# Casting loads on one queue, a causal triangle by matmul and a new instruction order in a fused chunk-selecting attention and softplus MLP kernel

## The chip, the core and the metric

The kernel runs on one core of a Trainium2 chip. The core has a matrix engine (PE, the weight loads of which the profile lists apart as PEld), a vector engine (DVE), a scalar engine (ACT), GpSimd (POOL) and a sync engine (SP) that only issues transfers here. POOL issues transfers too, on a queue of its own, and only POOL's transfers change the type of what they move. The engines run side by side, each in its own program order, and wait for one another on semaphores. The metric is the device time of one execution in microseconds, as a median over runs: 267.46 us before the change (three runs, 266.27 to 268.2).

## What is computed

The inputs are q, k, v of shape (4, 8, 768, 64), batch, heads, tokens and width, and two MLP weights of 512 x 2048 and 2048 x 512, all f32. Each head's 768 keys are cut into 24 chunks of 32. A query looks only at the six chunks whose upper bound of the score is largest, among the causal ones:

```python
ub = np.sum(np.maximum(q*k_min, q*k_max), axis=-1)          # per query and chunk
ub = np.where(causal, ub, -1e9)
top_chunks = np.argsort(ub, axis=-1)[..., -6:]
scores = scale * np.matmul(q, k.T)
scores = np.where(sel & (pos[:, None] >= pos[None, :]), scores, -1e9)
attn = softmax(scores);  x = attn @ v                        # heads side by side: 512 wide
h = x @ w_in
out = softplus(h) @ w_out                                    # 3072 x 512, f32
```

## The kernel before, in words

**Blocks.** The 3072 tokens are worked on in 12 blocks of 256 queries, numbered n; a block belongs to batch n // 3 and is the first, second or third part (k = n % 3) of that batch's 768 tokens. The eight heads are four pairs. Everything is bf16 in SBUF.

**Preparation of a block.** k and q are loaded with tokens on partitions and turned so that the width is on partitions (names kT and qT). In blocks 0 to 2 the turning is done by PE against an identity (L468 to L472, by groups of two pairs in block 0); from block 3 on by a transposing DMA on SP's queue (L473). From turned k come the chunk maxima and negated minima (L500, L502, DVE), put into a block-diagonal matrix BD (L505), and the keys themselves copied into KA and KB (L512). Turned q is copied (L535) and split in its positive and negative parts (L543). PE then makes the bounds (L565, name ub), DVE the sixth largest of each row and a raw mask (L588, L602), which is turned (L622 by PE, from block 3 on by DMA) and copied into spare rows of the q tiles (L644), so that the score matmul adds the mask by itself.

**Attention of a block.** For each pair and head, PE makes scores in pieces of two key tiles (L684 to L689), ACT exponentiates a piece into the tile pt (L695), POOL puts zeros above the diagonal of the two diagonal tiles with an affine_select (L703 to L707), PE multiplies by v with an extra column of ones (L712), DVE divides by the sum (L725) into the tile osb, and osb is turned into x: by PE and a copy in blocks 0 to 2 and 11 (L740 to L749), by a transposing DMA in the others (L732).

**MLP of a block.** Eight steps h of eight matmuls (L786, one line for all, L791), each followed by an exponential on ACT, and a logarithm for every two (L796, L801); then 2 x 4 steps y of four matmuls (L814, L816), an eviction to ysb and a store.

**Loads.** Block 0's k and q come as f32 on SP's queue, in halves of four heads, with two neighbouring tokens of a head side by side on one partition (512 bytes in one piece; load_pairs, L344). ACT or DVE then casts each half to bf16. Everything else comes as casting loads on POOL's queue: q, k, v of a block in two loads of 128 tokens (load, L328, pieces of 256 bytes), the weights in four loads each (L372, L381). The loads of block 3 wait for the last part of w_out. The helper in_turn (L460) undoes the pairs' order when the turned tile is copied.

**The order of the work.** Nothing in the instruction order is left to the hardware: a planner writes each engine's program. An operation has a list of engines with costs, inputs, buffers and a key, which is the time by which it is wanted; its due time is the smallest of its key and its successors' due times less its own cost (L144 to L146). The planner then plays the kernel through (L136): on each engine it takes, among the operations that could start within a tolerance of the earliest, the one that is due first. The keys hang on the table a (wanted starts of the blocks' attention), and on offsets for preparation, h, y and loads (PAR, L224). A transfer's landing is reckoned with one running end time per queue (L179 to L186). Buffers are counted in pools (sizes, L244): 8 for loaded q and k, 4 each for pt, osb and x, 2 for turned q.

**Fillers.** Before the weights are there, PE has little to do. keep_awake (L837) puts matmuls of zeros (L852, 128 x 128 by 128 columns) in the gaps of PE's planned program until 45 us or the first y step; they write a bank that nobody reads.

Of the kernel before, what the change touches and what calls it, by code (L numbers as in the profile page):

```python
# [10 lines left out]
BF16 = mybir.dt.bfloat16  # L11
# [52 lines left out]

class Op:
    __slots__ = ("name", "alts", "fn", "deps", "gate", "after", "succ", "alloc", "touch", "key",
                 "rel", "packet", "port", "due", "wait", "eng", "start", "end", "done", "dma", "n", "at", "inst")


class Plan:  # L70
# [5 lines left out]
    def op(self, name, alts, fn, deps=(), alloc=(), touch=(), key=None, dma=None, gate=(), after=(), rel=0.0, packet=19.0, port=False):  # L76
        o = Op()
        o.rel, o.packet, o.port = round(rel), packet, port
# [50 lines left out]
    @staticmethod  # L129
    def home_at(pool, s, e):  # L130
        t = 0.0
        for q, x, dma in pool.ends[s]:
            t = max(t, x + (LANDED[e] if dma else 0 if q == e == "PE" else LAT[q].get(e, 150)))
        return t

    def run(self, par):  # L136
# [7 lines left out]
        for o in reversed(topo):  # L144
            dur = min(c for _, c in o.alts) + (2500 if o.dma else 160)
            o.due = min([o.key] + [s.due - dur for s in o.succ])  # L146
        free = {"PE": 3000.0, "ACT": 2300.0, "DVE": 1000.0, "POOL": 800.0, "SP": 800.0}
        ring, packet = {"SP": 0.0, "POOL": 0.0}, {"SP": 19.0, "POOL": 32.0}
# [3 lines left out]
        while ready:  # L152
# [26 lines left out]
            if o.dma:  # L179
                other = "SP" if e == "POOL" else "POOL"  # L180
                at = max(o.end + (650 if e == "SP" else 1150), ring[e], 2650.0)
                back, part = max(0.0, ring[other] - at), packet[other] / o.packet
                ring[e] = at + o.dma + min(o.dma * part, back)
                ring[other] += min(o.dma, back / part)
                packet[e] = o.packet
                o.done = ring[e] + (450 if o.packet < 100 else 1000)  # L186
                if e == "SP":
                    o.end = max(o.end, ring[e] - 3500)
            else:
                o.done = o.end  # L190
# [4 lines left out]
            for b in o.touch:  # L195
                b.left -= 1
                b.ends.append((e, o.done, bool(o.dma)))
# [22 lines left out]
def dve(n, rate=1.0):  # L220
    return n / (0.96 * rate) + 66


PAR = dict(  # L224
    dmat=3,
    dmaT=450,
    narrow=1,
    l0=1,
    over="soy",
    maskD=3,  # L230
    awake=(1.06, 45.0, 5.7),
    first=(64.42, 64.23, 29.03, 95.39),
    loads=((87.43, 130.15, 71.7), 19.14, (76.86, 12.06, 15.17), 41.22),
    tol={"PE": 0, "ACT": 0, "DVE": 0, "POOL": 2358, "SP": 0},
    alt=636,
    ohd=(229.35, 150.58),
    a=(-46.8, -33.92, -31.03, -0.05, 17.1, 24.77, 54.71, 88.7, 133.12, 175.62, 173.66, 255.42, 297.45, 469.8),
    prep=((77.31, -48.97, -81.43, 46.38), (-8.14, 24.92, -67.86, -43.68), (53.78, -16.07, -58.0, 11.26), (25.03, -41.37, -16.45, 11.23)),
    av=(-0.8, 4.76),
    ot=(12.12, 10.86),  # L240
    hlag=(8.7, 27.7, 34.1, -3.53, 34.9, 33.84, 33.54, 32.2, 25.36, -32.32, 54.03, 77.81),
    ylag=(7.32, 7.87, 25.64, 26.35, 28.67, 47.05, 47.88, 49.45, 10.02, 22.03, 47.36, 37.39),
    ahead=(3.4, 19.67, 10.64, 22.05, 12.72, 9.33, 70.63, 47.4, 103.95),
    sizes=dict(s=2, h=2, y=1, o=1, t=2, xf=2, xp=4, kT=2, io=8, kx=2, q=2, pn=2, ub=2, pt=4, osb=4, x=4, g=2, e=4, ysb=4, mT=2),  # L244
# [3 lines left out]
def make_plan(T, par):  # L248
# [19 lines left out]
    P.op("zero", [("DVE", 80)], lambda e: nc.vector.memset(T.zero, 0.0), key=-100000)  # L268
# [26 lines left out]
    chunk_rows = [P.op("c4", [("POOL", 900)], f4, [r4], key=3000)]  # L295
    mr0, bd0, kb0, vone, ohk = [], [], [], [], {}
# [11 lines left out]
    for k0, k1 in ((0, 1), (1, NBLK)):  # L308
        for h in range(2):
            o = P.op("ohk", [("SP", 450)], lambda e, k0=k0, k1=k1, h=h: rows_of(0, k0, k1, h), oh[k0:k1],  # L310
                     key=par["ohd"][k0] * 1e3, dma=300 * (k1 - k0))
# [16 lines left out]
    def load(nm, n, when, gate=()):  # L328
# [6 lines left out]
        for t in range(NT):  # L335
# [4 lines left out]
                     gate=gate, key=key, rel=key - 2000 if n > 2 else 0.0, dma=950 if n < 3 else 2050, packet=32.0, **new)  # L340
            first = first or o
            ld[nm, n, t] = o

    def load_pairs(nm, n, when):  # L344
# [4 lines left out]
        for g in range(2):  # L349
# [4 lines left out]
                     key=1e3 * when[g], dma=950, packet=29.0, alloc=[st])  # L354
# [6 lines left out]
    def load_rows(nm, n, when):  # L361

        for t in range(NT):
            st = Buf(pool["xf"])
            d = P.op(f"ld {nm}{n}.{t}", [("SP", 560)], lambda e, t=t, st=st: nc.sync.dma_start(out=st.ap, in_=rows(nm, n, t)),
                     key=1e3 * (when + 0.3 * t), dma=1000, alloc=[st])
# [5 lines left out]
    def load_w_in(when):  # L372
        for c in range(4):
# [4 lines left out]
            w_in.append(P.op(f"w_in{c}", [("POOL", 800)], f, key=1e3 * (when + 0.4 * c), dma=2550, packet=173.0, after=w_in[-1:]))  # L378

    def load_w_out(when):  # L380
        for c in range(4):  # L381
# [4 lines left out]
            w_out.append(P.op(f"w_out{c}", [("POOL", 800)], f, key=1e3 * (when + 0.4 * c), dma=2550, packet=173.0,  # L386
# [5 lines left out]
    load_pairs("k", 0, (0.0, l0[0]))  # L392
    if par["l0"] < 2:
        load_pairs("q", 0, (l0[1], l0[2]))
    else:
        load("q", 0, l0[1])
# [4 lines left out]
    for nm, x in zip("kqv", l1):  # L401
        load(nm, 1, x)
    load_w_in(li)
    for nm, x in zip("kqv", l2):
        load(nm, 2, x)
    load_w_out(lo)
    for h in range(2):
        o = P.op("ohk", [("SP", 450)], lambda e, h=h: rows_of(1, 0, NBLK, h), oh, gate=[w_out[3]], key=40000, dma=900)
        for k in range(NBLK):
            ohk[1, k, h] = o  # L410
    kb0.append(P.op("kb0", [("SP", 450)], lambda e: nc.sync.dma_start(out=T.KB[1][0:32], in_=T.KB[0][0:32]), kb0[:1],
                    gate=[w_out[3]], key=40000, dma=600))
# [7 lines left out]
    for n in range(NB):  # L420
# [11 lines left out]
        for gi, ps in enumerate(groups):  # L432
# [14 lines left out]
            by_dma, pairs, qpairs = n >= par["dmat"], n == 0, n == 0 and par["l0"] < 2  # L447
# [20 lines left out]
            def transposes(nm, buf, t, n=n, ps=ps, p0=p0):  # L468
                o = t_of(buf)
                for p in ps:  # L470
                    nc.tensor.transpose(o[:, p - p0, t * 128:(t + 1) * 128],
# [476 lines left out]
```

## Time and profile before

| | us |
|---|---|
| median of three runs | 267.46 |
| the profiled execution, its own time | 266.59 |
| its span, first to last instruction | 264.8 |
| PE busy in it | 255.0 |
| ACT busy | 211.0 |
| DVE busy | 142.5 |
| POOL busy | 110.8 |
| fillers on PE (L852), 243 of them | 22.7 |

The span is what the page and the trace cut up; about 1.8 us of the execution lie around it. "Busy" joins the intervals of an engine's instructions. A matmul's interval includes its way through the array, so a row of short matmuls overlaps itself: its pace is read from how often one starts. A view by windows gives each engine's busy time in a stretch, with the granted clock of PE and the share of the DMA engines. In the timeline an entry in square brackets is the idle time of the engine just before that row, and what ended it. "To landing" is counted from the issue of a transfer until its data are there.

### The profile page before, as it was taken

What the parts mean: (1) busy time and instruction counts of PE and PEld (TensorE: products, weight loads), DVE (VectorE), ACT (ScalarE), POOL (GpSimd) and SP (SyncE); (2) the same over time, 40 slices, a digit from 0 to 9 for tenths busy, and PEclk for the clock granted to TensorE, in tenths of its full rate; (3) what the DMA queues carried; (4) which work ended last, traced back from release to release, by engine and by line L of the source; (5) the groups of instructions that cost most, each with busy time, mean ns of one, the idle gap of its engine ahead of it and who ended that gap; (6) DMA issues with size and microseconds to landing.
All of it is one profiled execution on the core that took longest, in us unless ns stands there. A gap on an engine that the chain in (4) does not pass through costs nothing.

```text
span 264.8 us, 7039 instructions
## 1 busy us (share of the span) xinstructions
PE 255.0 (96%) x2750; PEld 197.2 (74%) x2779; DVE 142.5 (54%) x500; ACT 211.0 (80%) x372; POOL 110.8 (42%) x193
## 2 busy tenths in 40 slices
PE   8698999999999999999999999999999999999995
PEld 8698898768775677788678864777888756887744
DVE  6589961019789667447634596584582164221012
ACT  3589999988687879999687992699997885999900
POOL 8927878798318520543990263401110211310000
PEclk9799999999999999999999999999999999999999
DMA  7996999999999984699699969624440123001022
GB/s 162 161 189 90 181 196 231 155 139 190 149 136 173 132 119 89 115 129 100 73 173 150 117 88 174 173 54 120 45 82 0 42 72 99 10 2 42 0 79 79
DMA packets 114719, 29.87 MB, mean 113 GB/s; under 512 B 104544, under 2 KB 111712, under 8 KB 114688
## 3 DMA queue, kind: packets, MB, share of 16 engines
q0 software_dynamic: 74944, 13.11, 66.5%
q1 hardware_dynamic: 39744, 16.33, 33.0%
q8 instruction: 21, 0.34, 0.6%
q14 instruction: 10, 0.08, 0.1%
HBM read 27.26 MB, written 6.29 MB: 127 GB/s over the span
## 4 chain that ended last, share of the span: by engine, by line
PE 86%; DMA 5%; DVE 3%; ACT 3%; issue 1%; POOL 0%; DVEq 0%; POOLq 0%
PE ph L791 30%; PE py L816 17%; PE pt L816 9%; PE po L717 7%; PE ps L687 5%; PE py L852 4%; PE ps L688 4%; DMA io<-in_k_dram 3%; DMA x<-osb 3%; PE pt L687 2%; PE pt L688 1%; PE pt L570 1%; ACT g L801 1%; PE ph L816 1%; ACT e L796 1%
## 5 line engine op out<-in xcount | busy, mean ns | idle before, releaser
L791 PE MATMUL ph<-x,w_in_sb 128*128 128x256 bf16 x768 | 91.8, 272 | 0.0
L705 POOL TENSOR_SCALAR_AFFINE_SELECT pt<-pt 128x256 bf16<-128x256 bf16 x96 | 39.5, 419 | 112.6 <-ACT pt L695 112.1
L791 PEld LDWEIGHTS <-w_in_sb 128*128 128x128 bf16 x768 | 73.6, 98 | 11.5 <-DMA w_in_sb<-in_moe_w_in_dram 0.5
L695 ACT ACTIVATE pt<-ps 128x512 bf16<-128x512 f32 (+1 forms) x134 | 69.9, 564 | 9.4 <-PE ps L688 8.8
L796 ACT ACTIVATE e<-ph 128x512 f32<-128x512 f32 x96 | 56.3, 606 | 12.5 <-PE ph L791 11.8
L816 PEld LDWEIGHTS <-g 128*128 128x128 bf16 x400 | 37.4, 98 | 31.4 <-ACT g L801 0.5
L816 PE MATMUL py<-w_out_sb,g 128*128 128x512 bf16 x231 | 57.8, 379 | 1.5 <-ACT ysb L258 0.2
L801 ACT ACTIVATE g<-e 128x1024 bf16<-128x1024 f32 x48 | 51.1, 1072 | 1.0
L695 ACT ACTIVATE pt<-pt 128x512 bf16<-128x512 f32 (+1 forms) x58 | 32.4, 584 | 0.6 <-PE pt L688 0.6
L717 PEld LDWEIGHTS <-pt 128*128 128x128 bf16 x672 | 26.8, 97 | 5.1 <-issue 0.6
L259 DVE COPY ysb<-py 128x512 f32<-128x512 f32 x12 | 8.3, 691 | 36.9 <-PE py L816 36.9
L717 PE MATMUL po<-v,pt 128*128 128x65 bf16 x610 | 26.4, 193 | 0.3 <-DVE osb L728 0.3
L816 PE MATMUL pt<-w_out_sb,g 128*128 128x512 bf16 x108 | 26.2, 379 | 0.2
L727 DVE RECIPROCAL rec<-po 128x4 f32<-128x4 f32 x43 | 7.6, 178 | 34.9 <-PE po L717 34.6
L490 DVE TENSOR_REDUCE kx<-kT 128x32 bf16<-128x1024 bf16 x18 | 21.0, 1209 | 8.9 <-DMA kT<-io 8.9
L852 PE MATMUL py<-zero 128*128 128x128 bf16 x243 | 22.7, 245 | 1.1 <-DVE zero L268 1.1
L339 POOL DMA_DIRECT2D v<-in_v_dram x24 | 21.6, 905 | 3.8 <-DMA io<-in_q_dram 1.5
L339 POOL DMA_DIRECT2D io<-in_k_dram x22 | 20.0, 910 | 5.7 <-DMA w_in_sb<-in_moe_w_in_dram 2.2
L339 POOL DMA_DIRECT2D io<-in_q_dram x22 | 19.9, 910 | 0.7 <-PE ph L791 0.6
L728 DVE TENSOR_TENSOR osb<-po,rec 128x256 bf16<-128x256 f32 x43 | 18.2, 424 | 2.7 <-DMA x<-osb 1.3
L852 PEld LDWEIGHTS <-zero 128*128 128x128 bf16 x243 | 18.3, 111 | 1.3 <-DVE zero L268 1.1
L687 PE MATMUL ps<-qa,ka 96*128 96x256 bf16 x71 | 18.3, 273 | 0.7 <-DVE qa L259 0.7
(99 smaller groups left out, 302.5 us busy)
## 6 DMA issues: line engine op xcount, KB each, us to landing
out_dram<-ysb SPq DMA_DIRECT2D x23, 256.0 KB, 2.4
v<-in_v_dram POOLq DMA_DIRECT2D x24, 128.0 KB, 7.6
io<-in_k_dram POOLq DMA_DIRECT2D x22, 128.0 KB, 7.2
io<-in_q_dram POOLq DMA_DIRECT2D x22, 128.0 KB, 7.1
w_out_sb<-in_moe_w_out_dram POOLq DMA_DIRECT2D x4, 512.0 KB, 8.0
w_in_sb<-in_moe_w_in_dram POOLq DMA_DIRECT2D x4, 512.0 KB, 9.6
xp<-in_k_dram SPq DMA_DIRECT2D x2, 256.0 KB, 3.2
xp<-in_q_dram SPq DMA_DIRECT2D x2, 256.0 KB, 6.3
```

The source lines that it names most:

```text
L339: lambda e, t=t: nc.gpsimd.dma_start(out=into(nm, n, t), in_=rows(nm, n, t)),
L490: nc.vector.tensor_reduce(kx.ap[:, :, j].rearrange("d p (t c) -> d t p c", t=NT), kT.ap.rearrange("d p x -> d (p x)").rearrange("d (t p c ...
L687: nc.tensor.matmul(sp.ap[:, 0:QB], kk[0:nr, p, j * 128:(j + 1) * 128], qq, start=True, stop=True)
L695: lambda e, sp=sp, pt=pt, h=h, j=j, w=w: nc.scalar.activation(pt.ap[:, h, j:j + 2].rearrange("k j c -> k (j c)")[:, 0:w], sp.ap[:, 0:w], A ...
L705: nc.gpsimd.affine_select(out=d, in_=d, compare_op=ALU.is_ge, fill=0.0, base=0, channel_multiplier=-1, pattern=[[0, 2], [1, 128]])
L717: nc.tensor.matmul(o[:, u, h], pt.ap[:, h, j, c0:c0 + 128], T.V[i][:, j, 2 * p + h, :], start=(j == 0), stop=(j == t0 + u))
L728: nc.vector.tensor_tensor(osb.ap[0], o[:, :, :, 0:D], osb.ap[1].to_broadcast([128, NT, 2, D]), op=ALU.mult)
L791: nc.tensor.matmul(o[:, j], T.w_in[:, dt, ft * 128:(ft + 1) * 128], x.ap[:, dt], start=(dt == 0), stop=(dt == KDM - 1))
L796: lambda e, hb=hb, eb=eb, f2=f2: nc.scalar.activation(eb.ap[:, f2 * 512:(f2 + 1) * 512], hb.ap, ACT.Exp),
L801: lambda e, eb=eb, g=g, f4=f4: nc.scalar.activation(g.ap[:, f4 * 4:(f4 + 1) * 4].rearrange("f j c -> f (j c)"), eb.ap, ACT.Ln, bias=1.0),
L816: nc.tensor.matmul(yb.ap[:, 0:c1 - c0], g.ap[:, f, u * 128:(u + 1) * 128], T.w_out[:, f, c0:c1], start=(f == 0), stop=(f == KFF - 1))
L852: z.fn = lambda e: T.nc.tensor.matmul(T.pools["y"].homes[0][:, 0:128], T.zero, T.zero, start=True, stop=True)
```

## The change

1. **All q, k, v as casting loads.** Block 0's k and q no longer come through SP and f32 tiles, but on POOL's queue (l0=3). The four casts of block 0 go.
2. **k and q of blocks 0, 1, 2 as token pairs.** One load of 1024 pieces of 512 bytes (written as 256) takes the place of two loads of 1024 pieces of 256 bytes. A pair's two heads then don't lie side by side, so PE turns one head at a time: 16 transposes of 64 x 128 for a block's k or q, where there were 8.
3. **Causal triangle by matmul in blocks 0, 1.** After each of the two diagonal score matmuls, a matmul of the identity and a tile tri (the large negative number above the diagonal) adds to the same bank; the 16 affine_selects of those blocks go. Block 2 and later ones keep theirs.
4. **Queue model with waits.** The planner reckons the two queues piece by piece (class Rings), with the waits between them, and lets POOL wait when seven of its transfers are under way. Costs of transfers are set anew, SP's transposes count 1300 ns instead of 1200.
5. **Order anew.** All keys are new, there is a table tweak that shifts the due times of some 190 named operations, the second engine of an operation is chosen sooner (alt 636 to 28 ns), ACT and DVE have a tolerance. Pools: loaded q and k 8 to 6, turned q 2 to 3, pt 4 to 5, osb 4 to 2, x 4 to 3.
6. **Fillers** are 512 columns wide where there is room, otherwise 128.

```diff
-    l0=1,
+    l0=3,
+    both=3,
+    tri=2,
-    tol={"PE": 0, "ACT": 0, "DVE": 0, "POOL": 2358, "SP": 0},
-    alt=636,
+    tol={"PE": 0, "ACT": 175, "DVE": 186, "POOL": 9276, "SP": 0},
+    alt=28,
-    loads=((87.43, 130.15, 71.7), 19.14, (76.86, 12.06, 15.17), 41.22),
+    loads=((69.69, 12.65, 7.35), 1.73, (16.1, 25.06, 195.99), 7.17),
-    a=(-46.8, -33.92, -31.03, -0.05, 17.1, ...
+    a=(-53.62, -40.62, -29.02, -27.6, 70.05, ...
-    sizes=dict(s=2, h=2, y=1, o=1, t=2, xf=2, xp=4, kT=2, io=8, kx=2, q=2, pn=2, ub=2, pt=4, osb=4, x=4, ...
+    sizes=dict(s=2, h=2, y=1, o=1, t=2, xf=2, xp=4, kT=2, io=6, kx=2, q=3, pn=2, ub=2, pt=5, osb=2, x=3, ...
+    tweak={"w_out1": 40.32, "w_out0": -65.28, ... "ld q1": -26.06, ... "ld k0": -19.38, ... "ld k1": -15.4, ... "ld q0": -15.57, ...
...
+    def load_both(nm, n, when):
+        b, k = blocks[n]
+        SBt[nm, n] = Buf(pool["io"])
+        o = P.op(f"ld {nm}{n}", [("POOL", 900)], lambda e: nc.gpsimd.dma_start(
+            out=both(SBt[nm, n].ap), in_=src[nm][b, :, k * QB:(k + 1) * QB].rearrange("h (s t) d -> s h t d", t=NT)),
+                 key=1e3 * when, dma=1536, packet=24.0, land=SKEW, alloc=[SBt[nm, n]])
...
+                    if whole[nm]:
+                        for h in range(2):
+                            nc.tensor.transpose(o[h * 64:(h + 1) * 64, p - p0, t * 128:(t + 1) * 128],
+                                                both(SBt[nm, n].ap)[:, 2 * p + h, t], T.ident)
+                        continue
...
+                        add = last and tri
+                        for c0, c1, x in ((0, QB, qq), (QB, w, qq[:, 1] if last else qq)):
+                            jj = j + c0 // QB
+                            nc.tensor.matmul(sp.ap[:, c0:c1], kk[0:nr, p, jj * 128:(jj + 1) * 128], x, start=True, stop=not add)
+                            if add:
+                                nc.tensor.matmul(sp.ap[:, c0:c0 + 128], T.ident, T.tri, start=False, stop=True)
...
-                    if last:
+                    if last and not tri:
...
+        if e == "POOL":
+            if len(self.slots) >= 7:
+                o.end = max(o.end, self.slots[-7].done - self.slots[-7].land + 200)
+            self.slots.append(o)
...
+        for w in (512, 128):
+            while True:
+                c = w / 1.2 if t < 1e3 * par["awake"][2] else mm(w)
+                if t + c > o.start - 60:
+                    break
```

More of the change, by code (lines that the diff above doesn't have):

```diff
@@ L179, in run @@
             if o.dma:
[L180 to L186, printed above, removed]
+                for x, y in rings.add(o, t - 2500.0):
+                    y += x.land
+                    if x is o or x.done != y:
+                        x.done = y
+                        for z in x.succ:
+                            z.at.clear()
                 if e == "SP":
-                    o.end = max(o.end, ring[e] - 3500)
+                    o.end = max(o.end, o.done - o.land - 3500)
             else:
@@ L238 @@
[L238 to L244, printed above, removed]
+    awake=(1.14, 45.0, 5.7),
@@ L391, in make_plan, with load_kq @@
     l0 = par["first"]
-    load_pairs("k", 0, (0.0, l0[0]))
+    def load_kq(nm, n, when):
+        (load_both if n < par["both"] else load)(nm, n, when)
+    if par["l0"] < 3:
+        load_pairs("k", 0, (0.0, l0[0]))
+    else:
+        load_kq("k", 0, 0.0)
     if par["l0"] < 2:
@@ L837, in keep_awake @@
 def keep_awake(T, order, par):
-    fill, free = [], 1e3 * par["awake"][0]
+    fill, free = [], max(1e3 * par["awake"][0], 140 + next(o.end for o in order if o.name == "zero"))
     for o in order:
```

187 lines of the change are left out of this document (131 added, 56 removed).

## The prediction

> **What bounds the kernel now.** I read the page's first parts, then the busy time by windows, then the timeline of the first 37 us, then the transfers' times to landing. The page says that PE is busy nearly all the time:
>
> ```profile
> span 264.8 us, 7039 instructions
> PE 255.0 (96%) x2750; PEld 197.2 (74%) x2779; DVE 142.5 (54%) x500; ACT 211.0 (80%) x372; POOL 110.8 (42%) x193
> ```
>
> But 22.7 us of that are fillers, which compute nothing. The windows tell where; the second table is of the fillers alone.
>
> ```profile
> 0.00:15.00 15.00, 11.70 (x137) 11.54 (x137) 10.10 (x28) 7.58 (x12) 13.99 (x28) 0.89 1.61 163
> 15.00:30.00 15.00, 13.78 (x251) 12.44 (x249) 13.47 (x50) 14.07 (x22) 8.87 (x17) 1.00 1.06 144
> 30.00:45.00 15.00, 15.00 (x206) 13.42 (x203) 8.16 (x39) 14.08 (x30) 12.26 (x21) 1.00 1.24 212
> 45.00:261.30 216.30, 214.29 (x2167) 159.82 (x2193) 109.98 (x384) 175.26 (x310) 75.65 (x130) 1.00 0.95 101
> ```
>
> ```profile
> 0.00:15.00 15.00, 9.94 (x93) 8.79 (x93) 0.89 1.61 163
> 15.00:30.00 15.00, 9.04 (x115) 7.00 (x115) 1.00 1.06 144
> 30.00:45.00 15.00, 3.74 (x35) 2.46 (x35) 1.00 1.24 212
> sum 261.30, PE 22.72 PEld 18.25; mean PE 5.68 PEld 4.56
> ```
>
> The reader is to see two kernels in one. From 45 us to 261.3 PE works 214.29 of 216.30 us without a filler: there at most 2.0 us can be won by any order. Before 45 us PE has 22.72 us of fillers and 4.5 us of idle time (45 less 11.70, 13.78 and 15.00), 27.2 us in which the weights, the loads or block 0 were not ready. So the change is worth what it does to the first 45 us, and costs what it breaks behind. There, from 15 us on, ACT is 14.07 and 14.08 of 15 us busy, so that stretch gets shorter mainly by starting earlier. A finer window of the start, and its timeline:
>
> ```profile
> 10.00:15.00 5.00, 5.00 (x73) 5.00 (x69) 3.27 (x12) 3.38 (x6) 4.86 (x8) 0.66 2.25 165
> ```
>
> ```profile
> 0.81 1.00 SPq L352 DMA_DIRECT2D xp<-in_k_dram  x2
> 2.08 1.90 POOL L339 DMA_DIRECT2D io<-in_k_dram  x2
> 4.66 0.63 PE L471 MATMUL pt<-ident,io 128*128 128x128 bf16 x4
> 7.67 0.62 ACT L258 CAST io<-xp 128x512 bf16<-128x512 f32 x1 [2.33 <-DMA xp<-in_q_dram]
> 9.50 0.62 PE L471 MATMUL ph<-ident,io 128*128 128x128 bf16 x8 [2.24 <-DMA io<-in_k_dram]
> 9.96 2.39 PE L852 MATMUL py<-zero 128*128 128x128 bf16 x23
> 10.64 0.62 ACT L258 CAST io<-xp 128x512 bf16<-128x512 f32 x1
> 12.13 0.63 PE L471 MATMUL ph<-ident,io 128*128 128x128 bf16 x4
> 13.41 0.22 PE L570 MATMUL ph<-bd,qpos 128*128 128x16 bf16 x1
> 15.22 0.17 PE L570 MATMUL pt<-bd,qpos 128*128 128x16 bf16 x1
> 27.55 0.77 POOL L376 DMA_DIRECT2D w_in_sb<-in_moe_w_in_dram  x1
> 28.31 1.05 POOL L705 TENSOR_SCALAR_AFFINE_SELECT pt<-pt 128x256 bf16<-128x256 bf16 x2
> 31.84 0.42 DVE L728 TENSOR_TENSOR osb<-po,rec 128x256 bf16<-128x256 f32 x1
> 36.06 1.03 PE L791 MATMUL ph<-x,w_in_sb 128*128 128x256 bf16 x8
> ```
>
> Block 0's k is turned from 4.66 us. Its q is late: the halves are cast at 7.67 and 10.64 us, and the first half's transposes stand behind block 1's k on PE, which waits 2.24 us for it, until 9.50. Then 23 fillers take 2.39 us, 104 ns each, at a granted clock that is down (0.66 from 10 to 15 us). So block 0's bounds, L570, begin at 13.41 for the first group and at 15.22 for the second. The first MLP matmul starts at 36.06 us: the first part of w_in is issued only at 27.55.
>
> **The change, part by part.** The prices come from these rows: transfers, counted from issue to landing, first by the page and then by the trace's extremes (minimum, median, maximum; the first line of extremes is that of v in the first 45 us, the second that of w_in), then the selects of the first 45 us, four PE transposes in the chain of waits, three waits from the list of waits, and the extremes of the transposing DMA of osb.
>
> ```profile
> xp<-in_k_dram SPq DMA_DIRECT2D x2, 256.0 KB, 3.2
> io<-in_k_dram POOLq DMA_DIRECT2D x22, 128.0 KB, 7.2
> DMA to landing us min/median/max: 4.8/6.4/11.8
> DMA to landing us min/median/max: 6.8/9.6/11.6
> L705 POOL TENSOR_SCALAR_AFFINE_SELECT pt<-pt x18: 396/408/579, 20.1 to 44.8; 128x256 bf16<-128x256 bf16 x18
> 33.81 0.22 PE pt L743 x4
> DVE osb L728 <- DMA x<-osb: 1.3, 1, 1.3
> PE po L717 <- DVE osb L728: 0.3, 1, 0.3
> POOL io L339 <- DMA w_in_sb<-in_moe_w_in_dram: 2.2, 1, 2.2
> DMA to landing us min/median/max: 2.3/2.7/7.0
> ```
>
> *The first loads.* Worked back from the code, the due times (successors' due less each cost, then tweak) are about -161 us for block 0's k, -158 for block 1's q, -157 for block 0's q, -149 for block 1's k; all can start at once, so POOL issues them in this order, each about 0.9 us, ahead of the identity, which is made at some 4.5 us and is still early enough. Lower bound for k: issued at 0.8 like SP's first, the shortest landing 4.8, and 0.9 us for twice the bytes (one more load of 128 KB at the spacing at which POOL issued two, 1.90 / 2): landed at 6.5. Upper bound: 0.8 + 7.2 + 0.9 = 8.9. Before, the first half's transposes ran at 4.66. So k is 2 to 4 us later; that costs nothing as long as q is the later one, as it was. q is third: 6.5 + 2 x 0.9 = 8.3 to 8.9 + 2 x 1.9 = 12.7; I take 9.5, nearer the low end, since SP's four f32 loads, 1 MB, no longer share the engines with POOL's. From transposes at 9.50 to bounds at 13.41 it took 3.9 us before, with PE at a low clock and the fillers ahead; from 12.13 to 15.22 it took 3.1. With 3.1: bounds at 12.6, for both groups at once, since one load brings all heads. Block 0 needs both groups; before, the second had them at 15.22. Gain 2.6, I take **2.5 us**; ends 0 (q at 12.7) and 3.8 (q at 8.3). If SP's casts go from ACT, 4 x 0.62 = 2.5 us of its work, I give nothing for it: they lay before 15 us, where ACT is busy 7.58 of 15 us. They are in the chain, and that is in the 2.5.
>
> The Trainium skill, DMA: Bandwidth & Descriptors, Anatomy of one DMA, gives a transfer of GpSimd's queue about 2.0 us plus its bytes at 436 GB/s. By that, an estimate, 256 KB issued by 1.7 us would be there at 4.3 and the gain would be near its upper end; the trace's 4.8 us minimum for half of that size speaks against it, and the measurement decides.
>
> *The triangle.* 16 selects of about 0.41 us go from POOL, and with them a stop between ACT and PE; 16 x 2 matmuls of 128 columns come, 55 ns each by the row of four in 0.22 us: 1.8 us of PE. In the rows above two selects start only at 28.31, when POOL has issued w_in: it is a queue behind transfers as well. What was behind each select is the pair's v matmul, the wait for which PE's fillers cover; only the last pairs of blocks 0 and 1 are on the way to x and to h. I take two such stops, 0.41 each and some queueing: **1.0 us** gained; ends 0 and 3.3 (half of the sixteen).
>
> *The weights.* By their due times the first part of w_out (-106) now goes before block 2's k and q (-55), and w_in's four parts (-45 to -28) right behind these, so that POOL reaches them at about 12 to 15 us instead of 27.55, with 16 selects no longer between. With 9.6 us to land, h could start 10 us sooner; but then x of block 0 is the late one, of which a late normalisation, L728, stood at 31.84, and which moves with the 2.5 us above. After 30 us there are only 3.74 us of fillers to be won, and ACT is full: I take **1.0 us**; ends 0 and 3.7. Seven transfers under way may hold POOL up; POOL's one wait of 2.2 us for w_in, ahead of a load, can be that kind of stop, and what is queued behind it here are the one-hot rows, v's ones and block 2's loads. Block 1's attention covers that.
>
> *The transposes by head.* 3 blocks x 2 x 8 = 48 more, at 55 ns 2.6 us of PE, with the triangle 4.4 us. All lie where the 243 fillers stand (93 + 115 + 35 by windows, 13.4 us even at 55 ns each) and give place. What counts is block 0's own chain, with 16 more transposes, 0.9 us, of which I take the half that is not beside copies of the other group: **0.4 us** lost; ends 0 and 4.4.
>
> *Small parts.* Block 0's keys were copied with the pairs undone, block 1's without:
>
> ```profile
> 8.78 0.58 ACT L258 COPY kb<-pt 64x512 bf16<-64x512 bf16 x1
> 20.41 1.01 ACT L258 COPY kb<-ph 64x1024 bf16<-64x1024 bf16 x1
> ```
>
> Blocks 1 and 2 now have six such copies of k and q; at 2 x 0.58 instead of 1.01 each they cost at most 0.9 us of ACT's time. A wider filler can hold up PE's next matmul, by four of 55 ns at most. I take zero, ends 0 and 0.9 lost.
>
> *After 45 us.* The order is new throughout, and osb has 2 buffers, x 3. At most 2.0 us can be won; what can be lost is a rival below. Zero.
>
> **The sum.** 2.5 + 1.0 + 1.0 - 0.4 = 4.1 us: a span of 264.8 - 4.1 = 260.7. The median stands 2.66 us above this span (267.46 - 264.8; the profiled execution's own 266.59 is 0.87 below the median). Forecast: 267.46 - 4.1 = **263.4 us**. With all upper ends, 3.8 + 3.3 + 3.7, it would be 256.7; they can't all come, since ACT is full from 15 us on, and I take 258 as the low end.
>
> **The rivals.** *B, the first loads eat the gain.* q lands at its upper bound, 12.7 us, and block 0's bounds come at 15.8, as before. For it: POOL's loads took 7.2 us at the median, SP's first ones 3.2. Against it: the 7.2 were seen while both queues were full. The first term is 0, the rest stays: 267.46 - 1.6 = 265.9 us, chance 0.19. The Trainium skill, DMA: Bandwidth & Descriptors, Issuing engine by pattern, calls SP's path generally faster than GpSimd's, and its Specifications put the line rate at 512 bytes and more; the trace agrees with the first (3.2 against 7.2), while no run yet shows whether 512 bytes read and 256 written count as large.
>
> *C, two osb buffers (slower).* In blocks 3 to 10 the third normalisation of a block needs the first osb back, and that is held until its transposing DMA has landed, 2.7 us at the median but 7.0 at worst. With four buffers DVE waited for it once, 1.3 us, and PE's v matmul 0.3. Block 3's four normalisations in the timeline began with the first and ended with the second of these rows:
>
> ```profile
> 83.66 0.42 DVE L728 TENSOR_TENSOR osb<-po,rec 128x256 bf16<-128x256 f32 x1
> 89.94 0.42 DVE L728 TENSOR_TENSOR osb<-po,rec 128x256 bf16<-128x256 f32 x1
> ```
>
> That is 2.1 us apart on average; two spacings, 4.2 us, cover the median landing and not the long one. If PE loses 1.3 us once in each of the 8 blocks, 10.4 us: 263.4 + 10.4 = 273.8 us. It decides from 0.85 us per block on (4.1 and 2.7 over 8). PE can do h and y steps meanwhile if the order has them there. Chance 0.16.
>
> *D, the added matmuls find no cover (slower).* The fillers were put by the plan; if the 80 added matmuls come after their stretch, or block 0's chain waits for each, 4.4 us are paid and nothing else comes: 267.46 + 4.4 = 271.9 us. Against it: after 15 us alone 150 fillers stood in the profile before, 8.3 us at 55 ns. Chance 0.09.
>
> **How the numbers follow.** Forecast 0.56 (its own range 258.5 to 264.8), B 0.19, C 0.16, D 0.09. One per cent, about what a measurement of this kernel can tell from no change, is 2.7 us: faster below 264.8, slower above 270.1. Faster: the forecast's 0.56 less 0.02 for its edge, and 0.03 of B: 0.57. Same: most of B, the edge, and weak cases of C and D: 0.19. Slower: 0.24. The range goes from 258 to 272.5: below it lie 0.05, above it most of C and a little of D, 0.13.
>
> **What would show it.** Right: no f32 tile xp; POOL's first load of k landed between 6.5 and 8.9 us; PE without an idle stretch of 2 us and the granted clock at 1.00 from about 6 us on; bounds of block 0 all by 13 us; the first L791 before 33 us; fillers under 19 us; PE busy 99% from the first y step on. B would show in bounds at 15 us or later, C in DVE waiting at L728 for x<-osb in most blocks and PE at L717 for DVE, D in a first MLP matmul at 36 us or later with fewer fillers. The prediction is wrong if the stretch after 45 us gives or takes more than 2 us, or if the first MLP matmul moves by more than 5 us.

## The result, and the profile after

| | before | after |
|---|---|---|
| median | 266.87 us (265.28 to 268.2, 4 runs) | 275.05 us (274.57 to 275.34, 4 runs) |
| ratio | | 1.0347, 95% interval 1.0298 to 1.0396 |
| span of the profiled execution | 264.8 us | 273.2 us |

The change makes the kernel 3.5% slower (263.4 us was forecast, 272.5 us was the upper end of the range). Some executions of the runs below came out slow, among them the profiled ones of e1_buffers2 (275.98 us), e3_thin_loads (267.08) and r0_same_slack (918, of which no idle time is given); the medians count them, the ratios leave them out, and for e1_buffers2 too few others are left for a ratio.

The page of after begins like this:

```profile
span 273.2 us, 6797 instructions
PE 253.7 (93%) x2644; PEld 187.7 (69%) x2677; DVE 138.8 (51%) x490; ACT 211.0 (77%) x375; POOL 103.4 (38%) x180
```

PE is busy for 1.3 us less than before, and the span is 8.4 us longer, so PE stands still for 19.5 us where it was 9.8. The windows of after, to be held against those of before (the fillers alone are in the second table):

```profile
0.00:15.00 15.00, 12.36 (x117) 6.41 (x119) 11.05 (x24) 7.24 (x11) 12.89 (x32) 1.00 1.18 118
15.00:30.00 15.00, 13.79 (x214) 11.00 (x216) 12.19 (x55) 13.79 (x26) 11.40 (x16) 1.00 1.49 186
30.00:45.00 15.00, 14.13 (x176) 11.74 (x178) 6.80 (x33) 14.00 (x27) 3.42 (x4) 1.00 1.49 197
45.00:269.20 224.20, 212.88 (x2141) 158.26 (x2168) 108.76 (x380) 175.25 (x311) 75.67 (x130) 0.99 0.89 96
```

```profile
0.00:15.00 15.00, 9.35 (x36) 3.63 (x37) 1.00 1.18 118
15.00:30.00 15.00, 3.77 (x21) 1.80 (x24) 1.00 1.49 186
30.00:45.00 15.00, 0.00 (x0) 0.00 (x0) 1.00 1.49 197
```

The first 45 us did what the change was to do: 13.1 us of fillers in place of 22.7, and PE still idle for 4.7 us. Behind 45 us PE is idle for 11.3 us (224.20 less 212.88) where it was 2.0. One window holds nearly all of it, first before, then after:

```profile
60.00:140.00 80.00, 78.96 (x864) 60.46 (x874) 53.22 (x193) 67.80 (x121) 41.69 (x66) 1.00 1.37 131
```

```profile
60.00:140.00 80.00, 69.66 (x782) 53.88 (x788) 58.98 (x217) 63.45 (x113) 41.16 (x64) 0.98 1.62 137
```

PE's idle time there is 1.0 us before and 10.3 us after. Some matmuls have no record in these two traces (29 of 2779 and 33 of 2677, by the weight loads on the pages), so small idle times in them are partly holes in the record. The first and longest of these gaps, in the chain of waits of after:

```profile
47.37 6.30 DMA io<-in_k_dram
53.69 8.17 DMA kT<-io
61.88 2.35 DVE kx L598 x2
64.35 0.43 DVE osb L840
64.83 0.40 PE pt L855 x2
```

and the same place in the timeline:

```profile
61.88 2.35 DVE L598 TENSOR_REDUCE kx<-kT 128x32 bf16<-128x1024 bf16 x2 [2.92 <-DMA kT<-io]
64.14 0.17 DVE L839 RECIPROCAL rec<-po 128x4 f32<-128x4 f32 x1
64.35 0.42 DVE L840 TENSOR_TENSOR osb<-po,rec 128x256 bf16<-128x256 f32 x1
64.83 0.40 PE L855 MATMUL pt<-ident,osb 128*128 128x128 bf16 x2 [2.99 <-DVE osb L840]
```

Read it from the bottom. PE waits 2.99 us for one normalisation, osb. That needs nothing that is late. But DVE works in fixed order, and two reductions of the next block's keys stand ahead of it; these wait 2.92 us for SP's transposing transfer kT, which took 8.17 us to land. The granted clock drops as well: after this gap it is 0.68 from 65 to 70 us.

```profile
65.00:70.00 5.00, 4.95 (x59) 3.96 (x59) 2.77 (x20) 3.02 (x6) 1.41 (x2) 0.68 2.01 156
```

The transfers from 60 to 140 us, issue to landing in the last column, before and then after; the queue line is POOL's (packets, MB, time of its packets as a share of 16 engines' time):

```profile
q0 software_dynamic: 31920, 4.02, 85.8%
x<-osb SPq DMA_TRANSPOSE x16, 4.3
kT<-io SPq DMA_TRANSPOSE x5, 8.5
qt<-io SPq DMA_TRANSPOSE x5, 7.5
mT<-mraw SPq DMA_TRANSPOSE x5, 4.8
```

```profile
q0 software_dynamic: 38076, 4.80, 113.0%
x<-osb SPq DMA_TRANSPOSE x16, 4.3
qt<-io SPq DMA_TRANSPOSE x6, 8.2
kT<-io SPq DMA_TRANSPOSE x5, 8.4
mT<-mraw SPq DMA_TRANSPOSE x5, 5.2
```

This is the pair of views that tells most. The transposes land equally late in both kernels, to within 0.7 us at the median, although POOL moves 0.8 MB more in this window after. Before, next to nothing on PE's path was waiting for them. After, they are waited for: the waits from 60 to 140 us (total, times, longest), of before one of DVE's longest for a transpose (that for qt is as long), then those of after. PE's only wait for DVE in that window of before is the one of 0.3 us that the prediction shows.

```profile
DVE kx L490 <- DMA kT<-io: 1.5, 1, 1.5
```

```profile
DVE osb L840 <- DMA x<-osb: 7.0, 6, 2.6
DVE kx L598 <- DMA kT<-io: 5.4, 3, 2.9
PE pt L855 <- DVE osb L840: 3.0, 1, 3.0
PE po L829 <- DVE osb L840: 2.4, 3, 1.6
PE pt L829 <- DVE osb L840: 1.9, 1, 1.9
PE ps L799 <- DVE qa L333: 1.5, 1, 1.5
```

### The profile page after: what moved, and what is told of

Read it like the earlier page. It is cut to its first block, busy times and chain, and to the rows that moved or that the text cites. A ratio compares the mean times of both kernels' runs of the same rounds, so it can differ in the third digit from the quotient of the medians.

```text
span 273.2 us, 6797 instructions
## 1 busy us (share of the span) xinstructions
PE 253.7 (93%) x2644; PEld 187.7 (69%) x2677; DVE 138.8 (51%) x490; ACT 211.0 (77%) x375; POOL 103.4 (38%) x180
## 4 chain that ended last, share of the span: by engine, by line
PE 54%; DMA 26%; POOL 8%; DVE 6%; issue 2%; ACT 2%; SPq 0%; POOLq 0%; DVEq 0%
PE ph L903 20%; PE pt L928 11%; PE py L928 9%; DMA w_out_sb<-in_moe_w_out_dram 7%; DMA kT<-io 6%; DMA io<-in_k_dram 4%; DMA x<-osb 4%; PE ps L799 4%; PE po L829 4%; DMA io<-in_q_dram 2%; PE pt L799 2%; DVE kx L598 2%; ACT pt L807 2%; PE ph L928 2%; DMA mT<-mraw 2%
## 5 line engine op out<-in xcount | busy, mean ns | idle before, releaser
L903 PE MATMUL ph<-x,w_in_sb 128*128 128x256 bf16 x768 | 94.5, 274 | 0.0
L807 ACT ACTIVATE pt<-ps 128x384 bf16<-128x384 f32 (+1 forms) x140 | 73.7, 574 | 9.0 <-PE ps L799 7.8
L817 POOL TENSOR_SCALAR_AFFINE_SELECT pt<-pt 128x256 bf16<-128x256 bf16 x80 | 32.2, 421 | 108.9 <-ACT pt L807 108.6
L928 PE MATMUL py<-w_out_sb,g 128*128 128x512 bf16 (+1 forms) x206 | 50.6, 370 | 1.0
L928 PE MATMUL pt<-w_out_sb,g 128*128 128x512 bf16 x133 | 32.5, 379 | 0.6
L799 PE MATMUL ps<-qa,ka 96*128 96x256 bf16 (+1 forms) x134 | 23.3, 259 | 2.2 <-DVE qa L333 1.5
L799 PE MATMUL ps<-qt,kb 128*128 128x256 bf16 (+1 forms) x146 | 25.2, 257 | 0.0
L799 PEld LDWEIGHTS <-ka 96*128 96x128 bf16 x192 | 17.1, 98 | 8.2 <-issue 2.6
L418 POOL DMA_DIRECT2D io<-in_k_dram x18 | 16.3, 903 | 13.0 <-PE ph L903 9.3
L840 DVE TENSOR_TENSOR osb<-po,rec 128x256 bf16<-128x256 f32 x43 | 18.3, 424 | 4.8 <-DMA x<-osb 3.4
L799 PEld LDWEIGHTS <-kb 128*128 128x128 bf16 x192 | 16.6, 97 | 3.3 <-issue 0.2
## 6 DMA issues: line engine op xcount, KB each, us to landing
w_out_sb<-in_moe_w_out_dram POOLq DMA_DIRECT2D x4, 512.0 KB, 16.1
```

Of the source, the lines that this page charges most:

```text
L418: lambda e, t=t: nc.gpsimd.dma_start(out=into(nm, n, t), in_=rows(nm, n, t)),
L799: nc.tensor.matmul(sp.ap[:, c0:c1], kk[0:nr, p, jj * 128:(jj + 1) * 128], x, start=True, stop=not add)
L807: lambda e, sp=sp, pt=pt, h=h, j=j, w=w: nc.scalar.activation(pt.ap[:, h, j:j + 2].rearrange("k j c -> k (j c)")[:, 0:w], sp.ap[:, 0:w], A ...
L817: nc.gpsimd.affine_select(out=d, in_=d, compare_op=ALU.is_ge, fill=0.0, base=0, channel_multiplier=-1, pattern=[[0, 2], [1, 128]])
L840: nc.vector.tensor_tensor(osb.ap[0], o[:, :, :, 0:D], osb.ap[1].to_broadcast([128, NT, 2, D]), op=ALU.mult)
L903: nc.tensor.matmul(o[:, j], T.w_in[:, dt, ft * 128:(ft + 1) * 128], x.ap[:, dt], start=(dt == 0), stop=(dt == KDM - 1))
```

## The experiments

Four theories were set against each other. T1: the new order was laid out by a queue model whose landings the chip doesn't hold while POOL's loads run; DVE and PE stand in fixed order behind SP's transposes. T2: the two osb buffers (the prediction's rival C). T3: the wait for the second weight's last part makes block 3 late. T4: the added matmuls (rival D). "Order frozen" means that the planner's order of the kernel is kept instruction by instruction and only what is named is changed. PE's idle time from 60 to 140 us is 80 us less its busy time in that window.

| run | median, us | before beside it | ratio, 95% interval | PE idle 60 to 140, us |
|---|---|---|---|---|
| before | 266.87 | | | 1.0 |
| after | 275.05 | 266.87 | 1.0347 (1.0298 to 1.0396) | 10.3 |
| f_both | 267.28 | 265.68 | 1.0056 (1.0018 to 1.0093) | 0.8 |
| e1_buffers2 | 275.85 | 264.60 | | 8.0 |
| e2_no_gate | 276.87 | 265.68 | 1.0404 (1.0327 to 1.0480) | 8.5 |
| e2b_late_gate | 274.63 | 264.60 | 1.0334 (1.0255 to 1.0414) | 7.7 |
| e5_thin_v | 270.72 | 264.60 | 1.0135 (1.0051 to 1.0218) | 4.9 |
| e3_thin_loads | 264.20 | 265.68 | 0.9940 (0.9896 to 0.9985) | 3.9 |
| e6_thin_from3 | 261.79 | 265.41 | 0.9877 (0.9833 to 0.9921) | 0.0 |
| c_before_thin | 265.20 | 264.60 | 1.0022 (0.9986 to 1.0057) | 0.5 |
| r0_same_slack | 274.05 | 264.94 | 1.0321 (1.0250 to 1.0391) | |
| r1_slack_1500 | 272.48 | 264.94 | 1.0292 (1.0235 to 1.0349) | 8.9 |
| r2_slack_2500 | 269.54 | 264.94 | 1.0193 (1.0161 to 1.0224) | 3.7 |
| r4_slack_4000 | 271.31 | 264.94 | 1.0249 (1.0214 to 1.0284) | 6.0 |
| r5_slack_both | 271.35 | 265.41 | 1.0221 (1.0129 to 1.0313) | 3.8 |
| r6_slack_both | 273.22 | 265.41 | 1.0314 (1.0259 to 1.0369) | 4.4 |

**The parts without the new order (f_both).** The loads, the transposes by head and the triangle are put into the order of before by hand, at the places of what they replace:

```diff
-    lambda e, t=t: nc.gpsimd.dma_start(out=into(nm, n, t), in_=rows(nm, n, t)),
+    lambda e, t=t: load_both(nm, n) if n < WHOLE and nm != "v" else nc.gpsimd.dma_start(out=into(nm, n, t), in_=rows(nm, n, t)),
...
+    if add:
+        nc.tensor.matmul(sp.ap[:, c0:c0 + 128], T.ident, T.tri, start=False, stop=True)
...
-    order = keep_awake(T, order, PAR)
+    order = keep_awake(T, parts(T, order), PAR)
...
+WHOLE, TRI = 3, 2
```

> The kernel before with its own instruction order, into which parts 1 to 3 of the change are put by hand: block 0's k and q as casting loads of token pairs first on POOL's queue, blocks 1 and 2 likewise where their first load stood, transposes head by head, the triangle by matmul in blocks 0 and 1 and the 16 selects left out; fillers make place for the added matmuls as the plan allows. Queue model and order stay. Theory 1: the parts alone cost little or win a little, 264 to 268 us against 267 (the fixed order keeps the MLP's start where w_in lets it). Theory 4 (the added matmuls find no cover): 269 to 273 us.

The parts cost 0.6% (0.2 to 0.9%), and PE's window from 60 to 140 us is as full as before, 0.8 us idle:

```profile
60.00:140.00 80.00, 79.19 (x865) 60.53 (x875) 51.61 (x195) 68.30 (x121) 41.10 (x65) 1.00 1.21 122
```

So rival D is out, and the loss comes with the order (and with what goes with the order: the smaller pools and the times of the loads).

**More buffers (e1_buffers2).** `widen` hands the buffers out anew, in the frozen order. The unused tiles xf and xp are given up for it: with them (e1_buffers) 210.4 KB of each partition are needed where 207.9 are there, and that variant has no time.

```diff
-    sizes=dict(s=2, h=2, y=1, o=1, t=2, xf=2, xp=4, kT=2, io=6,
+    sizes=dict(s=2, h=2, y=1, o=1, t=2, xf=0, xp=0, kT=2, io=6,
...
+    widen(T, order, dict(osb=4, x=4, io=8))
```

> The changed kernel, its order frozen as it is, with more room: 4 buffers of osb in place of 2, 4 of x in place of 3, 8 of io in place of 6, and none of xf and xp. T1 (the order was laid out without slack against landings of SP's transposing DMAs that the chip doesn't hold while POOL's loads run): the waits of osb on the transfer of x go (3 waits, 7 us by the waits of after), but PE, ACT and DVE work in the same order, and pt and ps wait for the landings themselves: the time stays within 2 us of the 275.0 us of after. T2 (the two osb buffers are the price): 6 us or more back, at most 269 us.

The list of its waits from 60 to 140 us has no osb waiting for x any more, and PE waits for the same DVE steps; what stands behind them now is kT, mT and qt:

```profile
DVE kx L598 <- DMA kT<-io: 8.2, 3, 3.1
PE pt L855 <- DVE osb L840: 3.7, 1, 3.7
DVE qa L333 <- DMA mT<-mraw: 3.7, 1, 3.7
```

The four executions took 271.52, 275.72, 275.98 and 277.45 us. T2 allowed at most 269, so the two osb buffers aren't the loss; that they are a part of it, up to the 3 us by which the fastest stands under after's fastest (274.57), isn't excluded. DVE's longest wait for a transfer, 7.0 us in after, was mostly no price: DVE came to the next late landing instead (kT, 8.2 us in place of 5.4).

**Without the wait for the weight (e2_no_gate, e2b_late_gate).** The first lifts all waits for the second weight's last part, the second, shown here, that of block 3's loads alone:

```diff
-        for d in o.gate:
+        for d in ([] if o.name.startswith("ld") else o.gate):
```

> The changed kernel's order kept; only the wait of block 3's loads and of three of SP's transfers for the last part of w_out is taken out, so POOL can issue block 3's first load at 34 us instead of 43.3. Theory 3 (the late weights hold block 3 up, and all later waits follow from this): block 3's keys are turned before 58 us instead of 61.9, PE's 3 us wait at 61.8 us goes, 5 to 10 us faster than the changed kernel. Theory 1: the loads only move the crowding; PE's first wait goes or shrinks, but the later ones (100 to 135 us) stay: 1 to 4 us faster. Theory 2: at most 1 us.

> The changed kernel, order frozen, with the wait on the last part of the second weight taken from the casting loads of block 3 alone; SP's three transfers keep it, so the stall at 15 to 30 us that the run without any such wait showed should not come. T1: the loads are issued some microseconds earlier, PE's stall at 60 us shrinks by up to 2 us, the later ones stay: 272 to 276 us. T3 (the wait for the weight's last part made block 3 late, and the rest follows): the 3 us gap at 60 us and most of what follows it go, at most 269 us.

The first brought a new stall with it: from 15 to 30 us PE was busy for only 10.47 us, waiting for loads of q and k beside which SP's three transfers now ran. With 276.87 us it met neither T3's expectation nor T1's, and it tells little by itself. The second has no such stall (14.66 us busy), and with 274.63 us it is as slow as after; PE still idles 2.2 us from 60 to 65 us. T3 is out.

**Thin loads.** If the competition with POOL's loads is what makes the landings late, less to load must bring them back, in the same order. Each of these fetches one head of eight for late blocks: e3 (shown) of blocks 6 to 11, c_before_thin likewise in the kernel before, e5 only v of these (`n >= 6 and nm == "v"`), e6 also k and q of blocks 3 to 5 (`n >= (6 if nm == "v" else 3)`). What isn't loaded is computed on stale data.

```diff
-        return src[nm][b, :, r0:r0 + 128].rearrange("h s d -> s h d")
+        return src[nm][b, 0:1 if n >= 6 else H, r0:r0 + 128].rearrange("h s d -> s h d")
```

> The changed kernel's order kept, but the loads of q, k and v of blocks 6 to 11 fetch one head of eight (blocks 6 to 11 thus compute on other data than the reference's); all other work is the same. Theory 1: without the crowd of loads SP's transposing DMAs land within 2 to 4 us, DVE's waits for kT, mT and x<-osb after 75 us shrink to under 4 us in all, PE's idle time from 70 to 140 us falls from 8 us to 2 or less: 5 to 8 us faster than the changed kernel, 267 to 270. Theory 2 (two osb buffers): the landing of x<-osb matters too, but kT and mT don't; 1 to 3 us. Theory 4 (rival D, the added matmuls): no change, 274 to 275.

> The changed kernel, order frozen, with only the loads of v of blocks 6 to 11 cut to one head of eight (it leaves out seven eighths of those loads); k and q land as they did. k and q are what SP's transposes read, v is read by nothing on SP. If the competition in the DMA engines is what makes SP's landings late (T1), a third of the bytes taken away gives back about a third to a half of the 10.9 us that all thin loads gave: 269 to 272 us. If it was the landings of k and q themselves that came late, v changes nothing: 274 to 276 us.

> The kernel before, order frozen, with the same edit as the run with thin loads (the loads of blocks 6 to 11 fetch one head of eight, so most of their work is done on stale data; it leaves out seven eighths of those loads). T1 in its sharp form: the order of before has slack against late landings, so it gains little from thin loads: 0 to 2 us, 264 to 267 us. If thin loads help any order of this kernel (less traffic is simply faster), before gains 6 us or more as well, and the run with thin loads says nothing about the new order.

> The changed kernel, order frozen, with the loads of k and q of blocks 3 to 5 thin too, beside all loads of blocks 6 to 11 (it leaves out seven eighths of those loads). The run with thin loads from block 6 on kept PE's first gap, 3 us idle at 61 us, since the loads in flight then are those of blocks 3 to 5. T1 (the same competition makes the first gap): the gap at 61 us shrinks to 1 us or less, PE idles under 2 us between 60 and 140 us, and the time is 260 to 262.5 us. If the first gap is another thing, such as the late start of block 3 behind the second weight's last part, it stays and the time is 263 to 266 us.

The transfers from 60 to 140 us of the last one, as above, and its window:

```profile
q0 software_dynamic: 6400, 0.76, 16.0%
x<-osb SPq DMA_TRANSPOSE x18, 2.6
kT<-io SPq DMA_TRANSPOSE x6, 3.9
mT<-mraw SPq DMA_TRANSPOSE x6, 2.5
qt<-io SPq DMA_TRANSPOSE x5, 3.2
```

```profile
60.00:140.00 80.00, 80.00 (x919) 63.16 (x916) 60.85 (x231) 74.32 (x134) 33.09 (x68) 1.00 0.58 92
```

Every landing takes 39 to 60% of the time in after, and PE doesn't stand still at all. In between lie e5 and e3, in the order of their bytes: 10.3, 4.9, 3.9 and 0.0 us of idle time. e5 touches only v, which nothing on SP reads, and gives 2.1% back: it is the competition, not the landing of what SP transposes. The first gap, at 61 us, stayed in e3 (PE waits 3.1 us there) and went in e6. That fits the same cause, but isn't parted from another: block 3's k itself is thin in e6, so its transpose is issued at 51.21 us in place of 53.69. And in the kernel before thin loads shorten the landings nearly as much, as the same view of c_before_thin shows:

```profile
q0 software_dynamic: 10341, 1.25, 26.3%
x<-osb SPq DMA_TRANSPOSE x16, 2.4
kT<-io SPq DMA_TRANSPOSE x6, 4.6
```

They bring nothing there, 1.0022. The lateness is in both kernels; only the new order pays for it. A limit of the comparison: c_before_thin is thin from block 6 on, as e3 is; e6 is thin from block 3 on for k and q and has no control of its own. And e3 came out faster than T1 had put it (264.20 us for 267 to 270).

**An order with slack.** T1 says that an order laid out with later landings should do better. The planner's keys, tweaks and tolerances were searched anew, blind to the chip, for several values of what the model adds between the last packet of a transpose and its landing: 0.3 us as in after (r0), 1.5 (r1, shown), 2.5 (r2), 4.0 (r4); r5 and r6 have 2.0 there and 2.3 for POOL's loads, which have 1.3 and 0.9 in after. The unused xf and xp are gone in all six.

```diff
-  ... dma=2 * par["dmaT"], packet=15.0, pen=11.0, land=300.0)
+  ... dma=2 * par["dmaT"], packet=15.0, pen=11.0, land=1500.0)
```

> Control for the three runs that follow. All parts of the change, full loads; the planner's keys and tweaks searched anew, blind to any run, with the queue model of the change as it is: 0.3 us from the end of a transposing transfer's packets to its landing. 321 of PE's 533 steps stand at another place than in after; the plan ends at 254.6 us, as that of after does (254.5). T1 (the order has no slack against landings that come 2 to 4 us later than planned while loads run): slow as after is, 270 to 277 us. If another draw of the order is all it takes (the loss is an accident of one order), this can as well come out at 264 to 267 us.

> The same search with one constant of the queue model changed: SP's transposing transfers land 1.5 us after their packets in place of 0.3 us. The plan ends at 254.5 us, the same as that of after, but each reader of such a landing stands 1.2 us later. T1: PE idles less between 60 and 140 us (10.3 us in after, 4 to 7 here) and the time is 266 to 271 us. If slack is not the cause, 273 to 277 us, as after and the control.

> The same search with 2.5 us in place of 0.3 us; the plan ends at 256.5 us, 2.0 later than that of after. T1: most of the lateness measured under load (2 to 4 us) is covered, PE idles 2 to 4 us between 60 and 140 us, and the time is 263 to 268 us although the plan is longer. If slack is not the cause, 2 us more than after: about 277 us.

> The same search with 4.0 us; the plan ends at 259.9 us, 5.4 later than that of after. T1: the slack now exceeds most of the lateness and its own price shows: 265 to 269 us, PE idle by at most 3 us between 60 and 140 us. If slack is not the cause, 5 us more than after: about 280 us.

> All parts of the change, full loads. The planner searched anew with room in both queues: SP's transposes land 2.0 us after their packets (0.3 in after), POOL's loads 2.3 us (1.3 and 0.9 in after). The plan ends at 255.9 us, 1.4 later than that of after and 0.5 earlier than that of the run with 2.5 us on SP alone. T1 in full (slack where loads and transposes meet, on either queue): PE idles at most 3 us between 60 and 140 us, 264 to 268 us, at least 2 us under the 269.5 us of that run. If only the room on SP counts: 269 to 271 us.

> The same model as the run before, from another start of the search; the plan ends at 256.0 us. It tells how far one order differs from another with the same slack. T1: 264 to 269 us, and within 2 us of its twin.

The order searched anew with the slack of after (r0, the control) is as slow as after, although 321 of PE's 533 steps changed places: no accident of one order. The plan with 2.5 us of slack is 1.9 us longer on paper than the control's and about 3.4 us shorter on the chip (1.0193 against 1.0321 of before, on the same chip), and the sign is what T1 says. But r1, r4, r5 and r6 came out above what T1 had put for them, r2 too by 1.5 us, and r6 is no better than the control (1.0314 and 1.0321). r5 idles as little as r2 in the window and is 1.8 us slower (each beside before: 1.0221 and 1.0193, whose intervals overlap). So slack on the landings may be worth some of the loss, 0 to 3.4 us of 8; with one order for each value, and 0.9% between the two orders of one model (r5, r6), that is suggested and not shown. One constant for it isn't the remedy: r2's x still landed after 4.0 us and its kT after 6.1. No order with the parts and the full loads was found that beats the kernel before.

## Why the prediction was wrong, step by step

**After 45 us, "Zero": the step that failed.** The prediction saw that at most 2.0 us could be won there and priced the loss only through osb's buffers. What is shown: 10.3 us of standstill from 60 to 140 us, which falls with the bytes that POOL loads beside it (e5, e3, e6) and isn't there when the same parts stand in the order of before (f_both). After and e6 have the same order and the same work on PE; between them lie 13.2 us of span (273.2 against 260.0). PE's idle time, the span less its busy time, makes up 11.7 of it (19.5 against 7.8; somewhat less in truth, since 33 matmuls of after have no record), and 1.5 us are PE's longer busy time, of which the clock of 0.68 after the first gap is one cause.

It could have been seen. The list of transfers of before has kT at 8.5 us to landing at the median, and the diff put the new model's constants beside each transpose: 2 x 480 ns of packets and 300 ns to land, with sharing among the two queues on top. For block 3's kT the list of steps that the changed kernel's planner makes has 5.1 us from issue to landing; it took 8.17. So it goes for all transposes that are issued from 60 to 140 us (median from issue to landing, in us, by the planner's list and by the trace):

| | before, planned | before, measured | after, planned | after, measured |
|---|---|---|---|---|
| kT | 7.7 | 8.5 | 4.3 | 8.4 |
| qt | 8.2 | 7.5 | 4.0 | 8.2 |
| mT | 6.2 | 4.8 | 3.6 | 5.2 |
| x | 5.0 | 4.3 | 2.5 | 4.3 |

The old planner's figures lie within 1.4 us of what was measured; the new one's are half of it to seven tenths. The prediction took the queue model as words, and didn't hold one of its constants against one row.

**Rival C named the place, not the cause.** DVE did wait at L840 for x<-osb, 6 times and 7.0 us, and PE for DVE. But with four buffers three of four executions were as slow as after and none came under 271.5 us. The 10.4 us it had priced are close to the loss by coincidence.

**The first loads, 2.5 us: mis-sized.** The first k was there earlier than the lower bound of 6.5: issued at 1.31, its first transpose ran at 5.86. Block 0's q was turned in two halves at 9.04 and 9.29 us, close to the 9.5 forecast. But the bounds of block 0 began at 14.38 and, in their second half, at 14.89, not at 12.6, and PE's first matmul there waited for POOL's copy of bd:

```profile
1.31 1.01 POOL L431 DMA_DIRECT2D io<-in_k_dram  x1 [0.80 <-POOLq L1047]
5.86 1.02 PE L576 MATMUL pt<-ident,io 128*64 128x128 bf16 x16
9.04 0.41 PE L576 MATMUL ph<-ident,io 128*64 128x128 bf16 x8 [0.29 <-DMA io<-in_q_dram]
9.29 0.39 PE L576 MATMUL pt<-ident,io 128*64 128x128 bf16 x8
14.38 0.17 PE L678 MATMUL pt<-bd,qpos 128*128 128x16 bf16 x1 [0.70 <-POOL bd L333]
14.89 0.17 PE L678 MATMUL ph<-bd,qpos 128*128 128x16 bf16 x1
```

Against 15.22 for the second group before, 0.3 us is won. The chain from q to the first bounds took 5.1 us, not 3.1: the copies, signs and bd of all heads stand between them. The idle stretches and the low clock are gone as forecast (1.00 in the first 15 us).

The Trainium skill, DMA: Bandwidth & Descriptors, Anatomy of one DMA, gave 2.0 us plus bytes at 436 GB/s, 2.6 us by the prediction's estimate; the first use came 4.55 us after the issue, and the measurement decides.

**The weights, 1.0 us: mis-sized the other way.** The first MLP matmul ran at 28.03 us in place of 36.06, and the first y step at 39.68 in place of 46.30. The prediction had called a shift of over 5 us a sign that it was wrong, and so it was: it let block 0's x hold the MLP back and move by the 2.5 us of the first loads alone. But block 0's last normalisation ran at 26.46 us in place of 31.84, and x was whole at 28.06, together with the first part of w_in (issued at 19.14, landed after 8.5). The parts of w_out took 16.1 us to land at the median (8.0 before), the last one until 42.81 us, and block 3's loads waited for it; but with that wait lifted (e2b) the time stayed.

**The transposes by head and the triangle.** With the loads they cost 0.2 to 0.9% in the order of before (f_both), which wasn't laid out for them; the forecast for the three was a gain of 3.1 us (2.5 + 1.0 - 0.4). Each alone wasn't tried. None of them makes the loss.

**The sum of the head's terms came near, by luck in part.** In e6, where the competition is mostly gone, the changed kernel stands 3.6 us under before (265.41 less 261.79); 4.1 us were forecast. But no term came as it was priced: 0.3 us at the bounds for 2.5, 8.0 us at the first MLP matmul for 1.0. And the added matmuls, priced at 0.4 us because fillers give place, are paid: beside c_before_thin, e6 has 8.6 us fewer fillers on PE (13.53 against 22.15) and 5.0 us more of other work (252.2 less 13.53 against 255.8 less 22.15). Between e6 and after lie 13 us.

What stays open: whether the shorter planned landings are the whole reason why the new order pays and that of before doesn't. The planner of r4 counts the transposes at 6.9 (kT), 6.9 (qt), 7.5 (mT) and 6.2 us (x), about as that of before does and longer than they then took (5.9, 3.7, 3.7 and 2.4), and PE still idles 6.0 us there, its longest wait one of 3.1 us for ACT. What none of the six new orders has is the time that the planner of before gives to POOL's loads: 27 us to landing at the median from 60 to 140 us, where 6.5 to 10.7 were measured, against 4.5 in after's list and 8.7 at most in theirs. That this room is what is missing is argued, not shown; no run has it.

## What to carry to other kernels

When a change lays an order anew by a model, check the model's constants against the landings of the old trace under load, before its plan: a plan that counts landings shorter than they are under load has its readers too early. A transfer that is late in both kernels is harmless until something in fixed order stands behind it, so look at who waits for a landing, not at how long it takes. And the longest wait in the list may be worth little: take it away, and the engine may come to the next late landing.

## What the runs showed of the hardware

SP's transposing transfers land in about half the time when few of POOL's casting loads run beside them: kT 3.9 against 8.4 us, qt 3.2 against 8.2, mT 2.5 against 5.2, x 2.6 against 4.3, with POOL's queue at 16.0% and at 113.0% of the engines' time. The Trainium skill, DMA: Bandwidth & Descriptors, Queues, rings and completion order, says that each DMA engine goes round the queues that have work, packet by packet; the halved times agree with that, and no run shows the turns themselves.

And a gap on PE can cost more than its length: that of 2.99 us in after was followed by a granted clock of 0.68 from 65 to 70 us, that of 3.1 us in e3 by 0.66. The length alone doesn't tell: in r1 PE idled 2.99 us from 75 to 80 us and had the full clock from 80 to 85 (1.00), in e2b it idled only 1.7 us from 95 to 105 us and had 0.66 from 100 to 105.
